# Top-k attention, routed experts and a gated feed-forward on one core: routing operands in one PSUM tile, row scaling a step ahead of its send

## The chip, the core and the metric

The kernel runs on one core of a Trainium2 chip: TensorE (PE, with its weight loads PEld), VectorE (DVE), ScalarE (ACT), GpSimd (POOL) and SyncE (SP, which here issues DMAs only). The metric is the device time in microseconds (us) of one launch. Three runs of the kernel before gave 615.75, 615.82 and 616.0 us; the median is 615.82 us.

## The reference

Three layers follow each other on 1152 tokens (2 batches of 576):

```
scores = q @ k.T / 8                      # 8 heads, head size 64
keep the 32 largest scores of each row, the rest to -1e9
attn = exp(scores - max);  attn /= sum(attn) + 1e-9
x = attn @ v                              # 1152 x 512
logits = x @ w_gate                       # 8 experts
e = argmax(logits);  gate = exp(0) / (sum(exp(logits - max)) + 1e-9)
pos = number of earlier tokens with the same e;  kept while pos < 288
y = relu(x @ w1[e]) @ w2[e] * gate        # 512 -> 1024 -> 512
h = y @ w_in;  out = (h * clip(h + 3, 0, 6) / 6) @ w_out   # 512 -> 2048 -> 512
```

## The kernel before

The attention works on 72 units. A unit is 128 query rows of one head: 9 row tiles `t` times 8 heads `h`, unit `u = 8t + h`. (Row tile 4 is made of the last 64 rows of both batches, so its units have twice as many products with v.) A software pipeline runs 72 steps; step `i` holds stages of several units, and within a step the letters of the string `STEP` give the order in which the instructions are written. Each engine takes its own instructions in that order, so the string is the queue of every engine. The letters that matter here:

- R: `round1(i+1)` and `merge(i-3)` on DVE: the eight largest of each of eight column chunks (L399), and for an older unit the merging of such lists into its 32 largest (L424, L426, L428).
- G: `rest(i)`: on POOL every eighth step the checks of `judge` (L434 to L437), on DVE every fourth step `norm` (L490 to L492: add 1e-9 to the row sum, reciprocal, product with the output of the attention), every eighth step `gate` (L511), and in some steps the parts of the routing.
- L: `round2(i-2)` on DVE (L417), one list over the whole row. It needs POOL's `drop_excess`.
- X, S, B: on POOL `excess(i)` (L405), `shift(i-3)` (L442) and `drop_excess(i-1)` (L413). `excess` of a step waits until `round2` of the step before has let go of its buffer.
- C, Z, F, M, E: on ACT `cut_excess` (L410), `shift_rest` (L447), `fetch` (L383), `below` (L451) and `expo` (L473). `shift` and `shift_rest` write one buffer: POOL takes the first 200 of 576 columns, ACT the other 376.
- T, A, Q: on PE the transposes through PSUM (L466, L467), the products with v (L484), and every second step the scores of two later units (L378). In eight early steps Q also multiplies v by the gate weights (`mix`, L501).
- V: on ACT, the step after a `mix`, the copy of its result into the v tile (`mixed`, L508), and once the copy of the token counts (L549).

When row tiles 0 to 5 are done, `route` gives their tokens an expert. Its parts are spread over steps: `pick` (step 56; L522 to L528), `weigh` and `count` (end of step 57: exp on ACT, 27 small matmuls on PE), `weight + place` (step 59; L552 to L559), and `choose` (steps 58, 60, 61, 62; L232 to L237), which finds the expert with most tokens, so that SP can load its weights. Then `scatter` of one row tile each in steps 60, 63, 66 and 69: ACT scales the rows by their gate (L582), POOL sends them to their places in DRAM (`send_rows`: a memset of a spacer, L154, and an indirect DMA, L155). Row tiles 4 and 5 are scattered behind the loop, with the last units and the routing of tiles 6 to 8. All operands of `route` lie in SBUF, apart from the counts, which TensorE writes to PSUM. PSUM buffers for counts, mixes and attention outputs come from one pool of two (`temp`, tag "o").

After the attention the eight experts and then the feed-forward follow; there the weights stream in on SP and TensorE multiplies.

Of the kernel before, what the change touches and what calls it, by code (L numbers as in the profile page):

```python
# [18 lines left out]
P = 128  # L19
# [16 lines left out]
STEP = "RGLXSCVBTAZFMEQ"  # L36
SPOOL = 200
# [9 lines left out]
CHOOSE = ((2, 0, 1), (4, 1, 1), (5, 2, 2), (6, 4, 2))  # L47
FIRST = 63
# [4 lines left out]
ROUTES = ((0, 6, 56, 3),)  # L53
# [9 lines left out]
def topk_attention_moe_ffn_kernel(ctx, tc, qT, kT, vx, vT, wg, w1, w2, w_in, w_out, out, cap):  # L63
# [20 lines left out]
    def forward(fast):  # L84
# [144 lines left out]
        def choose(sizes_now):  # L229

            v = nc.vector
            return [lambda: v.scalar_tensor_tensor(keys, sizes_now, float(E), rank, op0=OP.mult, op1=OP.add),  # L232
                    lambda: v.max(places, keys),
                    lambda: v.tensor_scalar(sums[:, 0], keys, places[:, 0:1], None, op0=OP.is_equal),
                    lambda: v.tensor_copy(whole[:1, :1], places[:1, :1]),
                    lambda: v.scalar_tensor_tensor(rank, sums[:, 0], float(FRONT), rank, op0=OP.mult, op1=OP.add),
                    lambda: v.tensor_scalar(eids[:, :1], whole[:1, :1], E - 1, E - 1, op0=OP.bitwise_and,  # L237
                                            op1=OP.bitwise_xor)]
# [5 lines left out]
        with ExitStack() as actx:  # L244
# [193 lines left out]

            def shift(u):
                t, h = divmod(u, H)  # L440
                x, top = ubufs[u % 2], tops[t][:, h, 0:1]
                nc.gpsimd.tensor_tensor(x[:, :SPOOL], top.to_broadcast([P, SPOOL]), st[u][:, :SPOOL], op=OP.subtract)  # L442

            def shift_rest(u):
                t, h = divmod(u, H)
                x, top = ubufs[u % 2], tops[t][:, h, 0:1]
                nc.scalar.activation(x[:, SPOOL:S], st[u][:, SPOOL:], AF.Identity, bias=top, scale=-1.0)  # L447

# [65 lines left out]
            def route(t0, t1, direct=False):  # L514
                n = t1 - t0
                r = lambda name, m=E: wk.tile([P, NT, m], F32, name=name, bufs=1)[:, :n]
                mx, dl, el, cand, cm, gt, a, pr = (
                    r("mx", 1), r("dl"), r("el"), r("cand"), r("cm", 1), r("gt", 1), r("ra"), r("pr", 1))
# [12 lines left out]
                pp_of, chosen = [], []  # L531
# [672 lines left out]
```

## Time and profile before

| what | value |
|---|---|
| median of three runs | 615.82 us |
| the profiled execution, its own time | 614.31 us |
| span of its trace | 612.5 us |
| mean granted clock of TensorE in it | 0.988 of full |
| PE busy in the span | 585.3 us (96%) |
| DVE busy | 380.5 us (62%) |
| ACT busy | 358.2 us (58%) |
| POOL busy | 305.2 us (50%) |

The shares mix two stages. Up to about 250 us the attention runs and all engines work; behind that PE works alone and the others wait for it. The start times in the rows below are microseconds from the start of the span; a bracket at the end of a row tells how long the engine was idle before the instruction and what it waited for.

### The profile page before, as it was taken

What the parts mean: (1) busy time and instruction counts of PE and PEld (TensorE: products, weight loads), DVE (VectorE), ACT (ScalarE), POOL (GpSimd) and SP (SyncE); (2) the same over time, 40 slices, a digit from 0 to 9 for tenths busy, and PEclk for the clock granted to TensorE, in tenths of its full rate; (3) what the DMA queues carried; (4) which work ended last, traced back from release to release, by engine and by line L of the source; (5) the groups of instructions that cost most, each with busy time, mean ns of one, the idle gap of its engine ahead of it and who ended that gap; (6) DMA issues with size and microseconds to landing.
All of it is one profiled execution on the core that took longest, in us unless ns stands there. A gap on an engine that the chain in (4) does not pass through costs nothing.

```text
span 612.5 us, 12183 instructions
## 1 busy us (share of the span) xinstructions
PE 585.3 (96%) x4092; PEld 526.2 (86%) x4094; DVE 380.5 (62%) x1793; ACT 358.2 (58%) x689; POOL 305.2 (50%) x374
## 2 busy tenths in 40 slices
PE   8999999999989877999999999999999999999995
PEld 4788888888877666899999999989899999989994
DVE  5999999999999988410463433447655663222221
ACT  4999999988988787212233444546545553242222
POOL 7999999999987799200022323333343232040002
PEclk9999999999997899999999999999999999999998
DMA  8539100100000431585687997522322210020001
GB/s 265 187 104 324 61 18 2 38 2 1 2 2 19 184 127 53 178 322 200 242 315 273 370 350 291 198 67 71 104 79 94 70 35 2 1 103 1 1 1 56
DMA packets 18110, 73.65 MB, mean 120 GB/s; under 512 B 2527, under 2 KB 2783, under 8 KB 15863
## 3 DMA queue, kind: packets, MB, share of 16 engines
q1 hardware_dynamic: 16599, 68.07, 31.6%
q0 software_dynamic: 1440, 4.72, 1.9%
q8 instruction: 34, 0.56, 0.4%
q14 instruction: 37, 0.30, 0.2%
HBM read 63.35 MB, written 9.44 MB: 119 GB/s over the span
## 4 chain that ended last, share of the span: by engine, by line
PE 70%; DVE 24%; POOL 3%; ACT 1%; issue 1%; DVEq 0%; ACTq 0%; POOLq 0%
PE h L1096 16%; PE acc L1110 16%; PE hps L989 12%; PE yps L989 11%; DVE lists L399 7%; PE av L484 6%; DVE lists L417 5%; DVE l L426 4%; PE ps L378 3%; PE pt L466 3%; DVE tops L428 3%; POOL s L413 1%; PE pt L467 1%; PE xp L168 1%; DVE tops L424 1%
## 5 line engine op out<-in xcount | busy, mean ns | idle before, releaser
L399 DVE MAX8 lists<-s 128x8 f32<-128x72 f32 x576 | 118.6, 220 | 3.9 <-ACT s L383 3.9
L484 PE MATMUL av<-vt,pts 128*128 128x96 f32 (+1 forms) x800 | 100.7, 275 | 0.0
L1096 PE MATMUL h<-x2h,fw 128*128 128x384 f32 x384 | 98.2, 337 | 1.1 <-DVE x2l L1007 1.1
L413 POOL TENSOR_TENSOR s<-s,cut 128x576 f32<-128x576 f32 x72 | 92.2, 1281 | 4.1 <-ACT cut L410 3.9
L484 PEld LDWEIGHTS av<-vt,pts 128*128 128x128 f32 (+1 forms) x800 | 92.0, 184 | 2.4 <-issue 0.9
L1110 PE MATMUL acc<-fw,gh 128*128 128x512 f32 x288 | 89.5, 392 | 0.0
L405 POOL TENSOR_TENSOR s<-s,lists 128x576 f32<-128x576 f32 x72 | 83.8, 1165 | 10.4 <-DVE lists L417 7.0
L466 PE MATMUL pt<-ident,ub 128*128 128x128 f32 x355 | 72.5, 290 | 12.4 <-POOL ub L442 7.8
L989 PE MATMUL yps<-hT,wslot 128*128 128x192 f32 (+5 forms) x512 | 78.5, 302 | 0.0
L466 PEld LDWEIGHTS pt<-ident,ub 128*128 128x128 f32 x355 | 50.6, 142 | 32.3 <-POOL ub L442 11.7
L1096 PEld LDWEIGHTS h<-x2h,fw 128*128 128x128 f32 x384 | 70.2, 188 | 5.1 <-DVE x2l L1007 1.3
L989 PEld LDWEIGHTS yps<-hT,wslot 128*128 128x128 f32 x512 | 72.5, 190 | 0.6
L989 PE MATMUL hps<-xe,wslot 128*128 128x192 f32 (+5 forms) x512 | 72.5, 302 | 0.2 <-DVE whole L207 0.2
L989 PEld LDWEIGHTS hps<-xe,wslot 128*128 128x128 f32 x512 | 71.2, 190 | 0.7 <-issue 0.7
L467 PE MATMUL pt<-drop,lb 128*128 128x128 bf16 x355 | 65.7, 222 | 0.0
L1096 PE MATMUL h<-x2l,fw 128*128 128x384 f32 x192 | 64.6, 337 | 0.0
L1110 PEld LDWEIGHTS acc<-fw,gh 128*128 128x128 f32 x288 | 53.4, 188 | 8.2
L1099 ACT ACTIVATE g<-h,three 128x384 f32<-128x384 f32 x48 | 27.9, 581 | 55.6 <-PE h L1096 55.5
L1100 DVE SCALAR_TENSOR_TENSOR g<-g,h 128x384 f32<-128x384 f32 x48 | 26.5, 551 | 54.6 <-ACT g L1099 54.3
L1104 DVE TENSOR_TENSOR gl<-g,gh 128x384 fp32r<-128x384 f32 x48 | 27.4, 571 | 50.5 <-ACT gh L1103 50.5
L1103 ACT CAST gh<-g 128x384 fp32r<-128x384 f32 x48 | 24.6, 513 | 56.5 <-PE acc L1110 51.8
L451 ACT ACTIVATE lb<-s,tops 128x576 bf16<-128x576 f32 x71 | 55.3, 779 | 3.9 <-DVE tops L428 3.2
(429 smaller groups left out, 1060.6 us busy)
## 6 DMA issues: line engine op xcount, KB each, us to landing
wslot<-in_w_dram SPq DMA_DIRECT2D x15, 2048.0 KB, 8.5
raw<-in_w_in_dram SPq DMA_DIRECT2D x16, 512.0 KB, 3.6
raw<-in_w_out_dram SPq DMA_DIRECT2D x16, 512.0 KB, 6.4
xs<-x_tok SPq DMA_DIRECT2D x8, 576.0 KB, 9.4
vt<-in_vx_dram SPq DMA_DIRECT2D x8, 365.0 KB, 4.5
kt<-in_kT_dram SPq DMA_DIRECT2D x8, 288.0 KB, 4.0
vts<-in_vT_dram SPq DMA_DIRECT2D x8, 288.0 KB, 2.9
qt<-in_qT_dram SPq DMA_DIRECT2D x9, 256.0 KB, 5.6
```

The source lines that it names most:

```text
L399: yield lambda c=c: nc.vector.max(lists[t % 2][:, h, c], st[u][:, c * CW:(c + 1) * CW])
L405: nc.gpsimd.tensor_tensor(s2, s, lists[t % 2][:, h, :NCK, KEEP:].to_broadcast([P, NCK, CW]), op=OP.subtract)
L413: nc.gpsimd.tensor_tensor(st2[u], st[u], cuts.pop(u), op=OP.subtract)
L417: nc.vector.max(lists[t % 2][:, h, NCK], st2.pop(u))
L451: nc.scalar.activation(lbufs[u % 2][:, :S], st.pop(u), AF.Relu, bias=tops[t][:, h, TOPK - 1:], scale=-1.0)
L466: nc.tensor.matmul(pt[:, c], ubufs[u % 2][:, cs], ident, is_transpose=True, start=True, stop=False)
L467: nc.tensor.matmul(pt[:, c], lbufs[u % 2][:, cs], drop, start=False, stop=True)
L484: nc.tensor.matmul(av[t, g][rows, h % 4], pts[:, c, cols], vt[b, h // 2][:, at:at + VC], start=c == 0, stop=c == 4)
L989: nc.tensor.matmul(out, wb[:, k], m[:, k, :self.w], start=first and k == 0, stop=last and k == HP - 1)
L1096: nc.tensor.matmul(h2, fw[f][:, 0, a, k * P:(k + 1) * P], (x2h, x2l)[b][:, k, c * CH:(c + 1) * CH], start=n == 0, stop=n == len(ops) - 1)
L1099: nc.scalar.activation(g, h2, AF.Relu, bias=three)
L1110: nc.tensor.matmul(acc[j], g[a][:, j * P:(j + 1) * P], fw[f][:, 1, b], start=f == 0 and n == 0, stop=f == NF - 1 and n == 2)
```

## The change

- `norm` loses its add of 1e-9. The 65th row of the fifth chunk of v, which is padding, gets 1e-9 in the column of ones, and the padding of the transposed buffer gets a zero there, whose exponential is 1.
- In the loop `route` allocates one PSUM tile `board` of a whole bank when it is created, and keeps in it the maxima, the differences `dl`, the candidates, the place sums, the counts, and the operands of `choose` (keys, their maxima, the mark of the largest, its number). `gt`, `el`, `cm` and `ra` stay in SBUF. The two later routings use SBUF as before (`route(..., True)`).
- `route` starts at step 55 in place of 56. `weigh` is issued at the end of step 55, `count` at the end of 56, `weight + place` in step 57, and `choose` two instructions each in steps 58, 59 and 60. The scaling of a row tile comes at the end of steps 57, 60, 63, 66 and 69, its send at the end of the next step; five of the six are now inside the loop.
- `V` stands behind `F` in the order of a step.
- From unit 54 on POOL's `shift` takes 130 columns and ACT's `shift_rest` 446.

```diff
-STEP = "RGLXSCVBTAZFMEQ"
-SPOOL = 200
+STEP = "RGLXSCBTAZFVMEQ"
+SPOOL, SENDS = (200, 130), 54
...
-CHOOSE = ((2, 0, 1), (4, 1, 1), (5, 2, 2), (6, 4, 2))
-FIRST = 63
+CHOOSE = ((3, 0, 2), (4, 2, 2), (5, 4, 2))
+FIRST = 62
...
-ROUTES = ((0, 6, 56, 3),)
+ROUTES = ((0, 6, 55, 3),)
...
-        def choose(sizes_now):
+        def choose(sizes_now, free):
...
-            return [lambda: v.scalar_tensor_tensor(keys, sizes_now, float(E), rank, op0=OP.mult, op1=OP.add),
-                    lambda: v.max(places, keys),
-                    lambda: v.tensor_scalar(sums[:, 0], keys, places[:, 0:1], None, op0=OP.is_equal),
-                    lambda: v.tensor_copy(whole[:1, :1], places[:1, :1]),
-                    lambda: v.scalar_tensor_tensor(rank, sums[:, 0], float(FRONT), rank, op0=OP.mult, op1=OP.add),
+            key, top, this = (free[:, k] for k in range(3))
+            number = free[:1, 2, :1].bitcast(I32)
+            return [lambda: v.scalar_tensor_tensor(key, sizes_now, float(E), rank, op0=OP.mult, op1=OP.add),
+                    lambda: v.max(top, key),
+                    lambda: v.tensor_scalar(this, key, top[:, 0:1], None, op0=OP.is_equal),
+                    lambda: v.scalar_tensor_tensor(rank, this, float(FRONT), rank, op0=OP.mult, op1=OP.add),
+                    lambda: v.tensor_copy(number, top[:1, :1]),
...
+                nc.gpsimd.memset(u[:, S:S + 1], 0.0)
...
-                yield lambda: nc.vector.tensor_scalar(rs, o[:, :, VS - 1:VS], 1e-9, None, op0=OP.add)
-                yield lambda: nc.vector.reciprocal(rs, rs)
+                yield lambda: nc.vector.reciprocal(rs, o[:, :, VS - 1:VS])
...
-                mx, dl, el, cand, cm, gt, a, pr = (
-                    r("mx", 1), r("dl"), r("el"), r("cand"), r("cm", 1), r("gt", 1), r("ra"), r("pr", 1))
+                el, gt, a, cm = r("el"), r("gt", 1), r("ra"), r("cm", 1)
+                if direct:
+                    mx, dl, cand, pr = r("mx", 1), r("dl"), r("cand"), r("pr", 1)
+                else:
+                    board = temp([P, 6 * NT, E], "board")
+                    pp = board[:, :NT]
+                    dl, cand, *ones_of = (board[:, k * NT:k * NT + n] for k in range(1, 5))
+                    mx, pr = (x[:, :, :1] for x in ones_of)
...
-                               *[routes[at][i - at] for _, _, at, _ in ROUTES if i in (at, at + 3)],
+                               *[routes[at][i - at and 3] for _, _, at, _ in ROUTES if i in (at, at + 2)],
...
+                        if i == at:
+                            routes[at][1]()
                         if i == at + 1:
-                            routes[at][1]()
                             routes[at][2]()
-                        n, r = divmod(i - at - 4, gap)
-                        if r == 0 and 0 <= n < b - a:
-                            scatter(a + n)
-                            sent = a + n + 1
+                        n, r = divmod(i - at - 2, gap)
+                        if 0 <= n < b - a and r < 2:
+                            if r == 0 and i < NU - 1:
+                                rows[a + n] = wk.tile([P, DM], F32, name="xg", bufs=4)
+                                scale(a + n, rows[a + n])
+                            elif r == 1:
+                                send(a + n)
+                                sent = a + n + 1
...
+        vx[64, :, 4, (h + 1) * VS - 1] = 1e-9
```

How the change moves instructions shows at three places. The first is DVE's queue in the kernel before around step 61, where a `norm` meets two instructions of `choose` (`sums` marks the expert with most tokens):

```order
L428 MAX tops<-l_3373 128x8
L490 TENSOR_SCALAR rs<-av 128x4
L491 RECIPROCAL rs<-rs 128x4
L234 TENSOR_SCALAR sums<-keys,places 128x8
L492 TENSOR_TENSOR x_tok<-av,rs 128x288
L235 CAST whole<-places 1x1
```

In the changed kernel the same engine has a `norm` together with the six instructions of `weight + place` in step 57 (line numbers are those of the changed file):

```order
L562 TENSOR_REDUCE gt<-el 128x6
L563 TENSOR_SCALAR gt<-gt 128x6
L496 RECIPROCAL rs<-av 128x4
L564 RECIPROCAL gates<-gt 128x6
L567 SCALAR_TENSOR_TENSOR ra<-board,oh 128x48
L568 TENSOR_REDUCE board<-ra 128x6
L497 TENSOR_TENSOR x_tok<-av,rs 128x288
L569 SCALAR_TENSOR_TENSOR dest<-cm,board 128x6
```

The mark of the largest is gone from this norm (it stands with one neighbour in step 59), and the six instructions of `weight + place`, two steps earlier, share a step with a norm of one instruction less.

The second place is POOL's queue around the first send, in the kernel before (steps 59 to 61):

```order
L437 COPY rest_ok<-tops 128x8
L405 TENSOR_TENSOR s_3289<-s,lists_115 128x576
L442 TENSOR_TENSOR ub_203<-tops,s 128x200
L413 TENSOR_TENSOR s_3227<-s,cut 128x576
L405 TENSOR_TENSOR s_3335<-s,lists_115 128x576
L442 TENSOR_TENSOR ub_207<-tops,s 128x200
L413 TENSOR_TENSOR s_3289<-s,cut 128x576
L154 MEMSET spacer 1x1
L155 DMA xs<-xg,dest 9216x512
L405 TENSOR_TENSOR s_3396<-s,lists_115 128x576
```

And in the changed kernel (steps 57 to 59):

```order
L408 TENSOR_TENSOR s_3171<-s,lists_115 128x576
L448 TENSOR_TENSOR ub_203<-tops,s 128x130
L416 TENSOR_TENSOR s_3084<-s,cut 128x576
L408 TENSOR_TENSOR s_3222<-s,lists_115 128x576
L448 TENSOR_TENSOR ub_208<-tops,s 128x130
L416 TENSOR_TENSOR s_3171<-s,cut 128x576
L154 MEMSET spacer 1x1
L155 DMA xs<-xg,dest 9216x512
L437 TENSOR_TENSOR over<-lists_114 128x64
```

The first send has moved ahead of the checks of step 59, two steps earlier, and the shifts are narrower.

The third place is ACT's queue around a copy of a `mix` (`vt<-mix`), before:

```order
L410 ACTIVATE cut<-s_747 128x576
L508 COPY vt_126<-mix 128x8x8
L508 COPY vt_126<-mix 64x2x8
L447 ACTIVATE ub_207<-s,tops 128x376
L383 ACTIVATE s<-ps 128x576
L451 ACTIVATE lb_209<-s,tops 128x576
L473 ACTIVATE pts<-pt 128x640
```

And after:

```order
L413 ACTIVATE cut<-s_748 128x576
L453 ACTIVATE ub_208<-s,tops 128x376
L386 ACTIVATE s<-ps 128x576
L513 COPY vt_126<-mix 128x8x8
L513 COPY vt_126<-mix 64x2x8
L457 ACTIVATE lb_211<-s,tops 128x576
L479 ACTIVATE pts<-pt 128x640
```

The copies stand two activations later, and still ahead of the exponential (`pts<-pt`) of the same step.

## Rows read from the trace of the kernel before

**Rows 1.** The page: busy tenths of PE in 40 slices, the chain by engine.

```profile
PE   8999999999989877999999999999999999999995
...
PE 70%; DVE 24%; POOL 3%; ACT 1%; issue 1%; DVEq 0%; ACTq 0%; POOLq 0%
```

**Rows 2.** Windows: length, busy of PE, PEld, DVE, ACT, POOL (counts), PE clock, DMA.

```profile
120.00:140.00 20.00, 20.00 (x204) 16.61 (x202) 19.88 (x136) 17.47 (x32) 18.77 (x24) 1.00 0.01 2
...
186.00:191.00 5.00, 5.00 (x24) 3.75 (x23) 4.90 (x28) 4.53 (x9) 4.87 (x8) 0.50 0.00 0
...
222.00:232.00 10.00, 6.61 (x60) 5.97 (x60) 7.94 (x50) 7.92 (x14) 9.82 (x12) 1.00 0.01 2
```

**Rows 3.** Timeline of DVE: round2 of four steps (start, length, engine, line).

```profile
58.21 0.75 DVE L417 MAX8 lists<-s 128x8 f32<-128x576 f32 x1
...
82.83 0.75 DVE L417 MAX8 lists<-s 128x8 f32<-128x576 f32 x1
...
94.88 0.75 DVE L417 MAX8 lists<-s 128x8 f32<-128x576 f32 x1
...
119.17 0.75 DVE L417 MAX8 lists<-s 128x8 f32<-128x576 f32 x1
```

**Rows 4.** Timeline of DVE: the start of one norm.

```profile
168.59 0.15 DVE L490 TENSOR_SCALAR rs<-av 128x4 f32<-128x4 f32 x1
168.78 0.18 DVE L491 RECIPROCAL rs<-rs 128x4 f32<-128x4 f32 x1
```

**Rows 5.** Waits from 20 to 170 us: engine, line, waited for, total, times, longest.

```profile
ACT vt L508 <- PE mix L501: 3.4, 6, 0.7
DVE rs L490 <- PE av L484: 2.6, 3, 1.4
```

**Rows 6.** Timeline of DVE: instructions of routing and choice.

```profile
178.23 0.76 DVE L523 SCALAR_TENSOR_TENSOR dl<-L,mx 128x48 f32<-128x48 f32 x1
...
186.26 0.15 DVE L232 SCALAR_TENSOR_TENSOR keys<-pos_p,rank 128x8 f32<-128x8 f32 x1
...
189.37 0.24 DVE L553 TENSOR_SCALAR gt<-gt 128x6 f32<-128x6 f32 x1
...
189.76 1.18 DVE L557 SCALAR_TENSOR_TENSOR ra<-pos,oh 128x48 f32<-128x48 f32 x1
...
197.28 3.33 DVE L234 TENSOR_SCALAR sums<-keys,places 128x8 f32<-128x8 f32 x1
...
203.77 0.90 DVE L236 SCALAR_TENSOR_TENSOR rank<-sums,rank 128x8 f32<-128x8 f32 x1
...
240.74 1.00 DVE L528 TENSOR_TENSOR oh<-cand,cm 128x16 bf16<-128x16 f32 x1
```

**Rows 7.** Timeline of POOL beside them.

```profile
189.59 1.28 POOL L413 TENSOR_TENSOR s<-s,cut 128x576 f32<-128x576 f32 x1
...
197.69 1.17 POOL L405 TENSOR_TENSOR s<-s,lists 128x576 f32<-128x576 f32 x1
198.81 0.52 POOL L442 TENSOR_TENSOR ub<-tops,s 128x200 f32<-128x200 f32 x1
199.29 1.28 POOL L413 TENSOR_TENSOR s<-s,cut 128x576 f32<-128x576 f32 x1
...
219.79 0.99 POOL L155 DMA_INDIRECT xs<-xg,dest  x1 [0.16 <-issue]
...
240.55 1.15 POOL L744 TENSOR_TENSOR ub<-tops,s 128x576 f32<-128x576 f32 x1
```

**Rows 8.** Waits from 170 to 240 us, POOL's two.

```profile
POOL s L405 <- DVE lists L417: 5.9, 5, 1.5
...
POOL xs L155 <- DVE tops L428: 2.9, 2, 1.5
```

**Rows 9.** Timeline of ACT: a late shift.

```profile
206.06 0.61 ACT L447 ACTIVATE ub<-s,tops 128x376 f32<-128x376 f32 x1 [0.24 <-DVE tops L424]
```

**Rows 10.** Timeline of PE: the products with v of one unit.

```profile
185.34 2.39 PE L484 MATMUL av<-vt,pts 128*128 128x96 f32 x10
```

More of the change, by code (lines that the diff above doesn't have):

```diff
@@ L437, in judge, with spool @@
                 g.tensor_copy(rest_ok[:, 1, t], thr[:, :, 0])
+            def spool(u):
+                return SPOOL[u >= SENDS]
             def shift(u):
                 t, h = divmod(u, H)
-                x, top = ubufs[u % 2], tops[t][:, h, 0:1]
-                nc.gpsimd.tensor_tensor(x[:, :SPOOL], top.to_broadcast([P, SPOOL]), st[u][:, :SPOOL], op=OP.subtract)
+                x, top, n = ubufs[u % 2], tops[t][:, h, 0:1], spool(u)
+                nc.gpsimd.tensor_tensor(x[:, :n], top.to_broadcast([P, n]), st[u][:, :n], op=OP.subtract)
             def shift_rest(u):
                 t, h = divmod(u, H)
-                x, top = ubufs[u % 2], tops[t][:, h, 0:1]
-                nc.scalar.activation(x[:, SPOOL:S], st[u][:, SPOOL:], AF.Identity, bias=top, scale=-1.0)
+                x, top, n = ubufs[u % 2], tops[t][:, h, 0:1], spool(u)
+                nc.scalar.activation(x[:, n:S], st[u][:, n:], AF.Identity, bias=top, scale=-1.0)
             def below(u):
@@ L529, in route @@
                 ]
-                pp_of, chosen = [], []
+                at, chosen = [pos[:, sl]], []
                 def count():
-                    pp = temp([P, NT, E], "pos_p")
-                    pp_of.append(pp)
+                    to = temp([P, NT, E], "pos_p") if direct else pp
                     for t in range(t0, t1):
                         for j in range(t):
-                            nc.tensor.matmul(pp[:, t], ones, oh[:, j], start=j == 0, stop=False)
-                        nc.tensor.matmul(pp[:, t], tri, oh[:, t], start=t == 0, stop=True)
+                            nc.tensor.matmul(to[:, t], ones, oh[:, j], start=j == 0, stop=False)
+                        nc.tensor.matmul(to[:, t], tri, oh[:, t], start=t == 0, stop=True)
+                    if not direct:
+                        for j in range(t1):
+                            nc.tensor.matmul(to[:, t1], ones, oh[:, j], start=j == 0, stop=j == t1 - 1)
+                        chosen.extend(choose(to[:, t1], board[:, 5 * NT:5 * NT + 3]))
+                    at[0] = to[:, sl]
                     if direct:
-                        at[0] = pp[:, sl]
                         copy()
-                    else:
-                        for j in range(t1):
-                            nc.tensor.matmul(pp[:, t1], ones, oh[:, j], start=j == 0, stop=j == t1 - 1)
-                        chosen.extend(choose(pp[:, t1]))
-                at = [pos[:, sl]]
-                copy = lambda: nc.scalar.copy(pos[:, sl], pp_of[0][:, sl])
+                copy = lambda: nc.scalar.copy(pos[:, sl], at[0])
                 weigh = lambda: nc.scalar.activation(el, dl, AF.Exp)
@@ L583, in scale, with send @@
                                      scale=gates[:, t])
+            rows = {}
+            def send(t):
+                scat.append(send_rows(t, rows.pop(t)))
             def scatter(t):
-                xg = wk.tile([P, DM], F32, name="xg", bufs=4)
-                scale(t, xg)
-                scat.append(send_rows(t, xg))
+                if t not in rows:
+                    rows[t] = wk.tile([P, DM], F32, name="xg", bufs=4)
+                    scale(t, rows[t])
+                send(t)
             def all_in_order():
@@ L762, in in_steps @@
                 nc.scalar.copy(plain[:, :DM // 2].rearrange("p (h d) -> p h d", d=D), x_tok[:, t, :4, :D])
-                nc.vector.tensor_scalar(rs, o[:, :, VS - 1:VS], 1e-9, None, op0=OP.add)
-                nc.vector.reciprocal(rs, rs)
+                nc.vector.reciprocal(rs, o[:, :, VS - 1:VS])
                 nc.vector.tensor_tensor(x_tok[:, t, 4:, D:], o[:, :, D:VS - 1], rs.to_broadcast([P, 4, E]), op=OP.mult)
```

6 lines of the change are left out of this document (3 added, 3 removed).

## The prediction

> **What bounds the kernel now.** I read the page's slices and its chain first. PE is at least nine tenths busy in every slice from the seventeenth to the last but one and holds 70% of the chain; DVE holds 24%, nearly all of it in the attention [rows 1]. The change touches only the attention, up to 250 us. What follows is PE work without gaps, so I take every microsecond won or lost at the end of the attention to arrive at the end of the span.
>
> Then the windows. In the attention no engine is alone: from 120 to 140 us PE is busy for all 20 us and DVE for 19.88 (row tile 4, whose products with v are double). From 222 to 232 us POOL is busy for 9.82 of 10, DVE for 7.94, ACT for 7.92 [rows 2]. So the bound moves: DVE in general, PE in row tile 4, POOL at the end.
>
> DVE's pace is read from `round2` (L417), once a step. Eight steps take 24.62 us while `mix` runs (58.21 to 82.83) and 24.29 us behind it (94.88 to 119.17) [rows 3]. Eight steps hold two norms and one gate, some 1.7 us, so a bare step is 2.82 us. POOL's step is the excess (1.12 from its start to the shift's), the shift (0.48) and the drop (1.25): 2.85 us [rows 7], with sends and checks on top. The two are nearly equal, so a stall of one is made up only where the other waits.
>
> The stretch from 178 to 211 us is the one that matters. Small DVE instructions of the routing take many times their length there: L523 0.76 us, L557 1.18, L234 3.33, L236 0.90, while L232, which reads its counts from PSUM, takes 0.15 [rows 6]. L557 starts inside a POOL drop (189.59 for 1.28) and ends 0.07 us behind it. L234 starts before an excess and ends 0.04 us behind the drop that follows it, at 200.57 [rows 7]. A DVE instruction with all its tensors in SBUF here waits until POOL pauses; one with a PSUM operand does not. POOL in turn waits for DVE: its idle time before the excess is 5.9 us in five waits, and 2.9 us in two waits ahead of a send, whose row scaling ACT has not done [rows 8]. That is 8.8 us of POOL idle, and behind 211 us POOL never catches up.
>
> [...]
>
> **The change part by part.**
>
> *Adds of the norm.* L490 to L491 is 0.19 us [rows 4]; the reciprocal now reads PSUM, and by L232 against its neighbours that costs nothing visible. I count 0.19 per norm, only where DVE bounds. In steps 9 to 28 it goes with the moved copies (next). In steps 29 to 36 two norms: 0.4. In row tile 4 PE bounds: nothing, for what DVE saves it waits for PE (over the whole stretch L490 waits 2.6 us in three waits [rows 5]), save the one behind the last wait: 0.2. In steps 46 to 54 two norms, 0.4, but POOL, at 8 x 2.85 = 22.8 us and a set of checks in eight steps, stands close behind DVE's 23.9: I take 0.25. Together 0.85.
>
> *Copies of the mixes later.* ACT waits 3.4 us in six waits for PE's mix [rows 5] with the shift, the fetch and the exponential behind it; PE then waits for the exponential. After the move the shift and the fetch fill that wait. The eight steps could go from 24.62 to 24.29 - 2 x 0.19 = 23.9, 0.7 us in eight steps, over some 20 steps 1.7; if PE or ACT keeps the pace, 0. All engines then lie within 0.3 us of each other in four steps, so I take 1.2.
>
> *Routing and choice on PSUM.* POOL's idle time after the change, step by step. Step 55: five pick instructions at 0.2 each put DVE's round2, and POOL's next excess, 1.0 later. Step 57: 2.82 + norm 0.58 + six instructions at 0.2 = 4.6. One of the six, L563 (before: L553), is an add of SBUF to SBUF and still waits for POOL. Before it took 0.24, for POOL happened to pause [rows 6]; now POOL has its drop ready, and I find it 0.65 into that drop, so 0.65 us more (bounds 0 and 2.3, the rest of a whole POOL step). 5.25 against 2.74 of POOL: idle 2.4. Steps 58 on: choose costs 0.2 to 0.3 a step, and POOL, with sends, is the slower one. Idle together 3.4 instead of 8.8: 5.4 won.
>
> *Scaling a step ahead.* ACT scales as often as before, but by my count of the steps two to four us before POOL comes to the send. The waits of 2.9 us are in the 8.8. What is queued behind a send on POOL is the excess or the checks.
>
> *Five sends in the loop instead of four* before the last unit's drop: one send is 0.09 + 0.16 + 0.99 [rows 7], 1.2 us lost on POOL.
>
> *Narrow shift.* 200 columns take 0.52 us and 576 take 1.15 [rows 7], 1.68 ns a column, so 70 columns are 0.12 us; steps 57 to 71 save 15 x 0.12 = 1.75 us of POOL. ACT's shift of 376 columns takes 0.61 [rows 9], so its 70 more cost 0 to 0.11. ACT is busy for 7.92 us where POOL is for 9.82 [rows 2]: 2 us in ten are free, and 0.1 in a step of three is hidden by POOL; without that cover 15 x 0.1 = 1.5 us.
>
> *Board takes a PSUM buffer two steps earlier.* In step 57 the products with v must now wait for that step's norm; by the same count PE stands for about 3 us. PE has slack there, but before, behind the token counts, it ran at half clock from 186 to 191 us, ten products in 2.39 us [rows 2, 10]. A late exponential would hold ACT's cut and POOL's drop: 0 to 2.0 us lost, I take 0.65.
>
> *Tail.* The add of the last norm: 0.2 won. L528 waits behind POOL's full shift (240.55 + 1.15; 1.00 us [rows 6, 7]). That shift no longer follows a send, and the interleaved chain is one link shorter, so now an earlier link (`dl`) meets it: 0, bounds 0.9 won and 0.2 lost.
>
> *The two memsets of one column* fall before POOL has a unit to work on, and `FIRST` moves loads that come 50 us ahead of the first expert: nothing.
>
> Sum: 5.4 + 1.75 - 1.2 + 0.85 + 1.2 - 0.65 + 0.2 = 7.5 us won. The profiled execution took 614.31 us, so 606.8; the median of the runs is 1.5 above it, so 608.3 us.
>
> About eleven of the moved instructions now take a source from PSUM. [...]
>
> **The rivals.**
>
> 1. *The stall moves to the add that stayed in SBUF.* L563 meets a POOL that runs without a pause: L234 shows 3.3 us of such a wait. For it: its operands. Against: POOL's next excess waits for a round2 that stands behind L563, so POOL must pause within one step. With the upper bound, 1.65 more than counted, and 0 from the mix copies: 7.5 - 1.65 - 1.2 = 4.65, 611.2 us.
>
> 2. *More is won.* L563 slips between two POOL instructions (0.65), dl misses the shift (0.9), the mix stretch gives 1.7 (0.5 more), PE keeps its clock (0.65): 10.2 us, 605.6.
>
> 3. *The change does not do what it says*: POOL was the true bound before too. Then only its own queue counts: 1.75 - 1.2, and 0.2 in the tail: 0.75 won, 615.1. Against it: the 8.8 us of idle time.
>
> 4. *Slower: PE at half clock.* The pause in step 57 lets the clock fall and the small products of a step keep it there. At half clock a step is ten products at 2.39, about as much for the scores every second step, and for the ten matmuls of the transposes, which are shorter, I take 1.6: 5.2 us against POOL's 3.2 (2.74, a third of a send, an eighth of the checks). Each slow step costs 2.0; against the 8.15 won without clock loss, it decides from the fifth slow step. Six cost 12: 619.7 us. For it: clock 0.50 in 186 to 191. Against: it lasted about two steps, and in 222 to 232 PE is idle for a third of the time at full clock [rows 2].
>
> **How the numbers follow.** My forecast, 608.3, has a chance of 0.56 (606.5 to 610.3: clock, tail and mix copies each part of the way to their bounds). Rival 1: 0.20, rival 2: 0.11, rival 3: 0.06, rival 4: 0.07. The range of 605.2 to 612.6 takes in rivals 1 and 2 and leaves out 3 and 4 and part of the ends. Within 0.2% (1.2 us) is about what a measurement of this kernel cannot tell from no change. Faster by more: 0.56 + 0.20 + 0.11 = 0.87; the same: 0.06; slower: 0.07.
>
> **What would show it.** Right, if in the profile after the instruction that marks the largest key takes under 0.25 us, POOL's idle time before the excess and the sends falls below 4 us, no send waits for its scaling, and POOL's full shift starts 6 to 9 us earlier than 240.55 us [rows 7]. L563 at 0.5 to 1.0 us shows that term; above 1.5 is rival 1. Eight steps near 24.0 between 55 and 85 us show the copies; 24.6 shows that PE holds them. A clock at half for over 10 us between 180 and 215 us is rival 4. The forecast is wrong if POOL is busy without a pause from 185 us on and that shift still comes less than 4 us earlier, or if the time behind the attention changes by more than 1 us.

## The result and the profile after

The changed kernel takes 609.48 us (median of four runs, 608.93 to 609.91), the kernel before beside it 615.91 us (615.75 to 616.38): a ratio of 0.9894, 95% interval 0.9877 to 0.9911, 6.4 us won. The forecast was 608.3 us. The profiled execution of the changed kernel took 609.91 us with a span of 608.0 us. Two runs of the experiments at a mean granted clock of 0.557 and 0.655 (967.70 us of e3, 827.16 us of the kernel before) are left out of what follows.

The page after, busy tenths of PE and the chain by engine, answers to [rows 1]:

```profile
PE   8999999999989888999999999999999999999994
...
PE 75%; DVE 17%; POOL 5%; issue 1%; ACT 1%; DVEq 0%; POOLq 0%; ACTq 0%
```

DVE's part of the chain falls from 24% to 17% and PE's grows. Lines have moved: `round2` is now L420, the excess L408, the drop L416, the pick L534 to L540, the gates' sum L562 to L564, the places L567 to L569, the mark of the largest key L236.

Windows of the kernel after, columns as in [rows 2]:

```profile
58.00:82.00 24.00, 24.00 (x214) 20.57 (x212) 23.72 (x158) 23.16 (x45) 23.49 (x28) 1.00 0.25 80
...
120.00:140.00 20.00, 20.00 (x203) 16.61 (x202) 19.30 (x126) 17.47 (x31) 18.80 (x23) 1.00 0.01 2
...
181.00:186.00 5.00, 2.96 (x15) 2.87 (x16) 4.73 (x30) 3.19 (x7) 2.44 (x4) 0.61 0.00 0
```

From 58 to 82 us, where the mixes run, PE is now busy for all 24 us. In the kernel before, the same window read:

```profile
58.00:82.00 24.00, 23.69 (x212) 20.31 (x208) 23.79 (x157) 22.82 (x44) 23.50 (x28) 1.00 0.27 83
```

PE had 0.31 us to spare there, and the change used it up. `round2` of the four steps that answer to [rows 3], on DVE's timeline:

```profile
58.00 0.75 DVE L420 MAX8 lists<-s 128x8 f32<-128x576 f32 x1
...
82.32 0.75 DVE L420 MAX8 lists<-s 128x8 f32<-128x576 f32 x1
...
94.18 0.75 DVE L420 MAX8 lists<-s 128x8 f32<-128x576 f32 x1
...
118.10 0.75 DVE L420 MAX8 lists<-s 128x8 f32<-128x576 f32 x1
```

Eight steps take 24.32 us in the stretch of the mixes (24.62 before) and 23.92 behind it (24.29 before). The waits from 20 to 170 us that answer to [rows 5]:

```profile
ACT s L386 <- PE ps L381: 5.9, 10, 0.9
...
DVE rs L496 <- PE av L490: 3.6, 5, 1.6
```

The six waits for the mix are gone, and ACT waits for PE's scores instead: 2.5 of these 5.9 us lie between 20 and 90 us, where the kernel before had no such wait. DVE waits 1.0 us longer than before for the products with v, 0.8 of it behind 90 us. What DVE saved in row tile 4 turned into that wait.

Routing and choice on DVE's timeline, against [rows 6]:

```profile
174.39 0.21 DVE L535 SCALAR_TENSOR_TENSOR board<-L,board 128x48 f32<-128x48 f32 x1
...
181.12 0.59 DVE L563 TENSOR_SCALAR gt<-gt 128x6 f32<-128x6 f32 x1
...
181.85 0.17 DVE L567 SCALAR_TENSOR_TENSOR ra<-board,oh 128x48 f32<-128x48 f32 x1
...
188.80 0.22 DVE L236 TENSOR_SCALAR board<-board 128x8 f32<-128x8 f32 x1
...
233.90 1.06 DVE L537 SCALAR_TENSOR_TENSOR cand<-dl,desc 128x16 f32<-128x16 f32 x1
```

0.76, 1.18 and 3.33 us have become 0.21, 0.17 and 0.22. The first and the last of them ran beside a busy POOL; the 0.17 fell into a pause of POOL (181.68 to 183.71), so that e8 below has to show what it takes beside one. The add of the gates (L563), which stayed in SBUF, takes 0.59. In the tail the stall of 1.00 us at `oh` has become one of 1.06 at `cand`, an earlier link of the same chain.

POOL's timeline beside them, against [rows 7]:

```profile
180.40 1.28 POOL L416 TENSOR_TENSOR s<-s,cut 128x576 f32<-128x576 f32 x1
183.71 1.17 POOL L408 TENSOR_TENSOR s<-s,lists 128x576 f32<-128x576 f32 x1 [2.02 <-DVE lists L420]
...
185.77 1.28 POOL L416 TENSOR_TENSOR s<-s,cut 128x576 f32<-128x576 f32 x1 [0.53 <-ACT cut L413]
...
233.79 1.15 POOL L765 TENSOR_TENSOR ub<-tops,s 128x576 f32<-128x576 f32 x1 [0.16 <-DVE dl L535]
```

And POOL's waits from 170 to 240 us, against [rows 8]:

```profile
POOL s L408 <- DVE lists L420: 2.7, 2, 2.0
...
POOL xs L155 <- ACT xg L592: 0.4, 1, 0.4
```

5.9 us before the excess have become 2.7, and of 2.9 us before the sends 0.4 remains, before a send behind the full shift. The wait of 0.53 for the cut is new, as are 0.21 us for a later cut and 0.74 for DVE ahead of the last narrow shift. Counted whole, from the shift of unit 52 to the full one, POOL sits idle for 9.5 of 66.2 us before and for 5.3 of 60.1 after (windows, before first, columns as in [rows 2]):

```profile
174.31:240.55 66.24, 53.54 (x449) 45.71 (x447) 62.12 (x362) 55.09 (x94) 56.78 (x73) 0.92 0.21 81
```

```profile
173.64:233.79 60.15, 50.67 (x448) 44.16 (x446) 56.01 (x352) 54.09 (x94) 54.90 (x73) 0.94 0.24 93
```

So 4.2 of the 6.1 us won there are idle time, and 1.9 are work that POOL no longer does. L563 ends (181.71) 0.03 us behind the end of the drop at 180.40: it waited for POOL as the others had. The full shift starts at 233.79, 6.8 us earlier. Of the clock, against [rows 2, 10], the products with v:

```profile
183.04 2.42 PE L490 MATMUL av<-vt,pts 128*128 128x96 f32 x10 [2.22 <-DVE dest L569]
186.85 2.31 PE L490 MATMUL av<-vt,pts 128*128 128x96 f32 x10
```

PE pauses for 2.22 us and runs two units at about half clock (0.61 in the window above), then at full clock. The first matmul of the first expert, the milestone that the rest of the text uses, on PE's timeline:

```profile
249.39 10.64 PE L1009 MATMUL hps<-xe,wslot 128*128 128x192 f32 x64 [0.20 <-DVE whole L207]
```

In the profile before it starts at 255.68 us, 6.3 us later. From there to the end of the last matmul both profiles take the same time, 349.77 us before and 349.78 after. The last matmuls, before and after:

```profile
605.07 0.39 PE L1110 MATMUL acc<-fw,gl 128*128 128x512 f32 x1
```

```profile
598.78 0.39 PE L1130 MATMUL acc<-fw,gl 128*128 128x512 f32 x1
```

What lies behind them is 7.07 us before and 8.79 after, and 7.77 in a second profile of the kernel after (e12). So the spans of the two profiles (612.52 and 607.96 us) are only 4.6 us apart, where the medians are 6.4 apart.

### The profile page after: what moved, and what is told of

It reads as the page before. It is cut to its first block, busy times and chain, and to the rows that moved or that the text cites. A ratio compares the mean times of both kernels' runs of the same rounds, so it can differ in the third digit from the quotient of the medians.

```text
span 608.0 us, 12169 instructions
## 1 busy us (share of the span) xinstructions
PE 583.1 (96%) x4092; PEld 525.0 (86%) x4094; DVE 374.2 (62%) x1775; ACT 357.9 (59%) x689; POOL 303.3 (50%) x376
## 4 chain that ended last, share of the span: by engine, by line
PE 75%; DVE 17%; POOL 5%; issue 1%; ACT 1%; DVEq 0%; POOLq 0%; ACTq 0%
PE h L1116 17%; PE acc L1130 16%; PE hps L1009 12%; PE yps L1009 12%; PE av L490 7%; DVE lists L402 5%; PE ps L381 4%; DVE lists L420 4%; PE pt L472 3%; DVE l L429 3%; POOL s L416 2%; DVE tops L431 2%; PE pt L473 1%; PE pt L646 1%; POOL s L408 1%
## 5 line engine op out<-in xcount | busy, mean ns | idle before, releaser
L416 POOL TENSOR_TENSOR s<-s,cut 128x576 f32<-128x576 f32 x72 | 92.7, 1288 | 4.5 <-ACT cut L413 4.2
L408 POOL TENSOR_TENSOR s<-s,lists 128x576 f32<-128x576 f32 x72 | 84.4, 1173 | 6.6 <-DVE lists L402 3.3
```

The costliest lines, as they stand in the source:

```text
L408: nc.gpsimd.tensor_tensor(s2, s, lists[t % 2][:, h, :NCK, KEEP:].to_broadcast([P, NCK, CW]), op=OP.subtract)
L416: nc.gpsimd.tensor_tensor(st2[u], st[u], cuts.pop(u), op=OP.subtract)
```

## The experiments

Single runs of one kernel lie up to 5 us apart here, more than most parts of the change are worth; places in the trace repeat far better. (A good part of the scatter lies at the two ends: in the 14 profiles the first shift starts at 15.3 to 16.5 us, and behind the last matmul there are 7.1 to 8.8 us.) So each profile is also read by POOL's shifts, one for each of the 72 units, counted from the first shift of the same profile, and by the first matmul of the first expert. The table gives them as differences to the kernel after (its own: units 36, 52, 56, 60 and 71 at 123.72, 173.64, 190.45, 202.85 and 233.79 us, the first shift at 15.61, the matmul at 249.39). Medians are of four to six runs, ratios against the kernel before on the same chip; the kernel after has 0.9894.

| kernel | us | ratio to before, interval | u36 | u52 | u56 | u60 | u71 | first matmul |
|---|---|---|---|---|---|---|---|---|
| before | | 1 | +0.77 | +0.97 | -1.08 | +4.22 | +7.06 | +6.59 |
| e8_psum_alone | 611.48 | 0.9919, 0.9906–0.9933 | +0.79 | +1.06 | -1.56 | +1.19 | +2.77 | +3.43 |
| e1_sbuf | 611.25 | 0.9920, 0.9907–0.9933 | +0.01 | +0.03 | +0.32 | +1.63 | +1.66 | +1.67 |
| e3_wide_shift | 611.17 | 0.9923, 0.9910–0.9937 | +0.02 | +0.04 | +0.11 | +0.34 | +1.53 | +1.54 |
| e2_scale_late | 610.50 | 0.9916, 0.9902–0.9931 | -0.01 | +0.03 | +1.48 | +1.26 | +1.29 | +1.30 |
| e4_copies_early | 612.04 | 0.9936, 0.9922–0.9949 | +1.04 | +1.06 | +2.12 | +2.38 | +2.42 | +3.50 |
| e5_norm_add | 609.73 | 0.9893, 0.9875–0.9910 | +0.18 | +0.19 | +0.60 | +0.79 | +0.78 | +1.51 |
| e6_gate_sum | 610.01 | 0.9904, 0.9889–0.9918 | -0.03 | 0.00 | -0.47 | -0.70 | -0.69 | -0.68 |
| e7_tail_psum | 610.76 | 0.9908, 0.9891–0.9925 | -0.02 | +0.01 | -0.42 | -0.66 | -0.67 | +0.63 |
| e9_pos_later | 609.65 | 0.9888, 0.9869–0.9907 | +0.02 | +0.06 | -0.99 | +1.31 | +1.34 | +1.45 |
| e10_pos_tail | 607.88 | 0.9862, 0.9844–0.9879 | -0.02 | +0.01 | -1.00 | -1.25 | -1.25 | -2.11 |
| e11_narrower | 607.95 | 0.9875, 0.9851–0.9900 | +0.01 | +0.03 | -1.06 | -1.57 | -2.02 | -2.01 |
| e12_after_again | 609.61 | 0.9896, 0.9879–0.9912 | -0.03 | -0.01 | -0.02 | +0.16 | +0.15 | +0.16 |

The last row is the same kernel in another profile: up to unit 56 places repeat within 0.04 us, behind it within 0.17.

**Operands back in SBUF (e1).** The theory that the waits on small instructions were the loss, against the order alone.

```diff
...
-                    dl, cand, *ones_of = (board[:, k * NT:k * NT + n] for k in range(1, 5))
-                    mx, pr = (x[:, :, :1] for x in ones_of)
+                mx, dl, cand, pr = r("mx", 1), r("dl"), r("cand"), r("pr", 1)
...
+                    three_of = wk.tile([P, 3, E], F32, name="free", bufs=1)
...
-                        chosen.extend(choose(to[:, t1], board[:, 5 * NT:5 * NT + 3]))
+                        chosen.extend(choose(to[:, t1], three_of))
```

> The kernel after with the routing's and the choice's operands back in SBUF (only the counts stay in PSUM); its order, its narrow shift and its early scaling are kept. Theory (the gain of steps 53 to 71 comes from small vector instructions that no longer wait through GpSimd's instructions): rows of about 1 us or more come back at dl, cand, ra, pr, dest or the comparison of keys, GpSimd's idle time over 5 to 14 us between 170 and 206 us grows again to 6 to 8 us from 3.6, the first expert's first matmul starts 2.5 to 5 us later than at 249.4, and the time is 612 to 614.5 against 609.5 after and 615.9 before. Rival (it is the new order of the sends alone that took the idle time away): the matmul starts within 0.8 us of 249.4 and the time is 609.3 to 610.3.

DVE's timeline and POOL's waits (170 to 240 us) of this kernel:

```profile
174.70 1.13 DVE L532 SCALAR_TENSOR_TENSOR dl<-L,mx 128x48 f32<-128x48 f32 x1
...
190.02 2.75 DVE L236 TENSOR_SCALAR free<-free 128x8 f32<-128x8 f32 x1
```

```profile
POOL s L408 <- DVE lists L420: 4.8, 4, 2.0
```

The waits return at `dl` and at the mark, POOL idles 2.1 us longer before its excess, and 1.67 us are lost: more than the rival allows, less than the 2.5 to 5 expected. Of the instructions put back in the loop only these two met a busy POOL. The 1.67 us are a net figure. The place sums are back in SBUF too, so ACT's copy of the counts no longer waits for DVE's last routing instruction, and POOL's waits for the cut fall from 0.7 to 0.2 us. And PE kept its full clock in this profile, after a pause of 2.29 us:

```profile
181.00:186.00 5.00, 2.71 (x27) 2.43 (x28) 4.76 (x31) 4.18 (x9) 2.97 (x4) 1.00 0.00 0
```

**Operands alone on the kernel before (e8).** After's `route` and `choose` in the kernel before; order, widths, sends and norms as they were.

> The kernel before with one part of the change alone: the routing's and the choice's operands in one PSUM tile, with the counts read where they were added up. The order, the wide shift, the scaling at the send and the two instructions of the norm stay as before. Theory (the port waits were most of the idle time before the sends): the waits of 1.18, 3.33, 0.90 us are gone, GpSimd's idle time between 170 and 220 us falls from about 8.8 us to 5 or 6, the first expert's first matmul starts 2.5 to 4 us earlier than at 255.7, and the time is 611.5 to 613.5. Rival (without the new order the sends still wait for the gather of dest and for the scaled rows, so nothing is won): the matmul starts within 1 us of 255.7 and the time is 615 to 616.

What the expectation calls port waits was seen only by its times: in the kernel before L523, L557, L234 and L236 end 0.02 to 0.07 us behind the end of a POOL drop, and no run shows a port. Against the kernel before the shift of the last unit starts 7.06 - 2.77 = 4.3 us earlier, the first matmul 3.2 us. The time is at the edge of the theory's range. Here the product that took 1.18 us (`ra`) meets a POOL drop, as in the kernel before, and takes 0.17 (DVE, then POOL):

```profile
189.41 0.17 DVE L564 SCALAR_TENSOR_TENSOR ra<-board,oh 128x48 f32<-128x48 f32 x1
```

```profile
189.24 1.28 POOL L415 TENSOR_TENSOR s<-s,cut 128x576 f32<-128x576 f32 x1
```

One wait of a send for its scaled row is still there (POOL's waits, 170 to 240 us; ACT's scaling ends at 195.59, the send starts at 195.89):

```profile
POOL xs L155 <- DVE rs L492: 1.8, 1, 1.8
```

So the operands are worth 1.7 us where the rest of the change is in and 4.3 where it is not: much of the idle time could be had in either way. The ratios say the same: the operands alone win 0.81%, all the rest without them 0.80%, both together 1.06%. The tail of this run lost 1.1 us to a half clock (below).

**Shift as wide as before (e3).** `SPOOL, SENDS = (200, 200), 54`.

> The kernel after with the late shifts as wide on GpSimd as before (200 columns in every step, not 130 from step 54). Theory (GpSimd sets the pace of steps 54 to 71, 18 shifts, each of 70 columns more): 1.3 to 2.2 us are lost, all of them after 180 us, the time is 610.8 to 611.7. Rival A (ScalarE, 10.00 of 10 us busy from 206 us on in the kernel after, is as much the bound): the time stays within 0.6 us of 609.5. Rival B (ScalarE is the bound and 130 is too narrow): 0.5 to 1.5 us are won, 608 to 609.

1.54 us lost, growing by 0.11 to 0.13 a unit from unit 59 to 69. POOL sets the pace there; rivals A and B fall.

**Scaling in the step of the send (e2).** The early `scale` is left out, `scatter(a + n)` scales and sends.

> The kernel after with the rows scaled in the step of their send, as before, not a step ahead. Theory (each send then waits for its scaled rows: two such rows of 1.5 and 1.4 us stood in the kernel before, on GpSimd, which has no slack there): 1.0 to 3 us of idle time of GpSimd with ScalarE's scaling as its releaser come back between 183 and 225 us, the first expert's first matmul starts 1 to 3 us after 249.4, and the time is 610.5 to 612.5. Rival (the scaling is done before GpSimd gets to the send anyhow): the waits for the scaled rows are under 0.5 us in all, and the matmul starts within 0.5 us of 249.4.

On POOL's timeline the first send shows it:

```profile
189.00 1.16 POOL L155 DMA_INDIRECT xs<-xg,dest  x1 [2.26 <-DVE lists L402]
```

What the send lacked is the row that ACT scales: that instruction ran from 187.99 to 188.70 us, so the releaser named in the row is not the one. It cost 1.5 us at unit 56, and no later send waited over 0.4 us. 1.30 us in all, at the low end of the theory, which had more than one such wait.

**Gate copies at their earlier place (e4).**

```diff
-STEP = "RGLXSCBTAZFVMEQ"
+STEP = "RGLXSCVBTAZFMEQ"
```

> The kernel after with the gate copies back at their earlier place in ScalarE's step. Theory by the trace after (TensorE itself bounds the steps with the mixes: it waits for nothing from 20 to 90 us, eight steps take 24.3 us, not 23.9; the later copies gave the 0.3 us between 24.62 and 24.32): eight steps from 58 us take 24.45 to 24.65 us, and the start of row tile 4 comes 0.3 to 0.8 us later; the time is 609.7 to 610.3. Rival (the copies' place costs nothing; the 0.3 us came from the shorter norm): eight steps stay at 24.3 us and all starts within 0.15 us of the kernel after.

Eight steps on DVE's timeline take 24.64 us, as the theory has it:

```profile
58.44 0.75 DVE L420 MAX8 lists<-s 128x8 f32<-128x576 f32 x1
...
83.08 0.75 DVE L420 MAX8 lists<-s 128x8 f32<-128x576 f32 x1
```

By unit 36 1.04 us are lost, the copies' whole worth in that stretch. Neither theory had what came at unit 56, 1.06 us more. The letter V also places ACT's copy of the token counts. First ACT's row, then POOL's:

```profile
183.97 0.20 ACT L559 COPY pos<-board 128x48 f32<-128x48 f32 x1 [2.91 <-DVE dest L569]
```

```profile
187.79 1.28 POOL L416 TENSOR_TENSOR s<-s,cut 128x576 f32<-128x576 f32 x1 [1.63 <-ACT cut L413]
```

That copy waits for DVE's last routing instruction on the shared tile; at the earlier place the shift, the fetch, a mask, an exponential, a scaling and then the cut are queued behind it, and POOL waits 1.1 us more for the cut.

**Add of the norm back (e5).** Two instructions in the loop's norm, as in the kernel before.

> The kernel after with the addition of 1e-9 back in the norm (two instructions of VectorE in place of one, in 17 norms before the tail; the data still holds the 1e-9). Theory (VectorE's saved instruction counts only where VectorE or a norm's product is late: my sum gave it 0.85 us): 0.5 to 1.1 us are lost, in steps 46 to 54 and in the first 30 steps, none in row tile 4 but 0.2 after its last wait; the time is 610 to 610.6. Rival A (VectorE bounds nearly every step outside row tile 4: 17 times 0.18 us): 2 to 3 us lost. Rival B (TensorE and GpSimd hide it all): under 0.3 us.

0.78 us by the last shift, as much as expected, but not where: 0.18 up to row tile 4, where it vanishes (-0.02 at unit 40), 0.19 at unit 52, and the rest in the steps around the first send, to which the theory gave nothing. The 0.73 more at the first matmul is mostly clock (below). The medians do not show the loss: 609.73 us, a ratio of 0.9893.

**Gates' sum in PSUM (e6).** One line: `gt = ones_of[0][:, :, 1:2]`.

> The kernel after with the sum of the gates (gt) moved to the same PSUM tile too. Theory (the row of 0.59 us of adding 1e-9 to gt is a wait for GpSimd): the row falls to about 0.2 us and the first expert's first matmul starts 0.2 to 0.5 us earlier than at 249.4; the time is 609.0 to 609.4. Rival (what follows it waits for something else anyhow): the row is shorter and nothing else moves, the time is 609.4 to 609.7.

```profile
181.64 0.17 DVE L564 TENSOR_SCALAR board<-board 128x6 f32<-128x6 f32 x1
```

That is the add, on DVE's timeline. 0.59 has become 0.17, and 0.47 us are won by unit 56, 0.70 by unit 60. The second part came with the clock: PE's pause is 1.8 us here, not 2.2, and one unit runs at half clock, not two. In the kernel after the scores behind the second slow unit come late and POOL's drop waits for the cut (ACT, then POOL):

```profile
190.42 0.65 ACT L386 ACTIVATE s<-ps 128x576 f32<-128x576 f32 x1 [1.25 <-PE ps L381]
```

```profile
196.51 1.28 POOL L416 TENSOR_TENSOR s<-s,cut 128x576 f32<-128x576 f32 x1 [0.21 <-ACT cut L413]
```

Neither wait is there in e6. The median (610.01) doesn't show the gain; its interval holds the kernel after's.

**Tail in PSUM (e7), on e6.** The tail's first `mx`, `dl` and `cand` in columns 384 to 432 of the PSUM tile that holds the products of heads 0 to 3.

> The kernel after with the sum of the gates in PSUM (measured before: 0.5 us) and, in the tail, the first routing's maximum, difference and candidates in unused columns of a PSUM tile that is there anyhow. Theory (the wait of 1.06 us at cand in the tail stands on the path to the first expert): cand takes about 0.2 us, the first expert's first matmul starts 1.0 to 1.6 us before 249.4, and the time is 607.9 to 608.6. Rival (as the stall moved from dl to cand by the change, it moves on to the next small instruction, or what follows waits for GpSimd's last shift anyhow): cand is short, but the matmul starts only 0.4 to 0.6 us earlier, as with the gates alone.

`cand` takes 0.17 us, and DVE has all that follows done 0.9 us earlier. But ACT's exponential of `dl` now reads that tile, and waits for DVE's last instruction on it:

```profile
235.95 0.18 ACT L571 ACTIVATE el<-av 128x16 f32<-128x16 f32 x1 [1.55 <-DVE x_tok L503]
```

With e6's 0.68 won before it, the tail loses 1.3, so for the matmul neither theory nor rival holds. Some 0.3 of it is that wait (the products of the last unit start at 240.70, in the kernel after at 240.38, the last shifts at 233.78 and 233.79). The rest is PE's clock at the last selection matmuls and the filler behind them, on PE's timeline:

```profile
247.94 1.36 PE L188 MATMUL ps<-wslot 128*128 128x192 f32 x4 [0.65 <-DVE xe L174]
```

In the kernel after those four take 0.92 us.

**Counts' copy a step later (e9, on e6), and cand with its addend in PSUM, dl in SBUF (e10, on e9).** The last three lines are e10's, of the tail alone; `base` gets a copy of `desc`.

```diff
-                                if i == at + 2:
+                                if i == at + 3:
                                     routes[at][5]()
...
+                    if at_psum is not None:
+                        cand = at_psum[:, :n * E].rearrange("p (n e) -> p n e", e=E)
+                        base = at_psum[:, n * E:n * E + E]
```

> The kernel after with the sum of the gates in PSUM (0.68 us won up to the last shift, measured before) and ScalarE's copy of the counts one step later. Theory (the copy waits 1.81 us, in ScalarE's queue ahead of a mask, an exponential, a scaling and the cut bits, for VectorE's last routing instruction on the same PSUM tile; the 0.53 us that GpSimd waits for the cut bits in that step hang on it): that wait of GpSimd goes, the last shift starts 1.0 to 1.3 us before that of the kernel after, counted from the first shift, the first expert's first matmul as much. Rival (VectorE's own queue bounds that step, as the 2.02 us that GpSimd waits for VectorE there say): 0.6 to 0.8 us, as with the gates alone.

> The one before, and in the tail only the candidates and a copy of their addend in unused columns of a PSUM tile; the difference, which ScalarE reads, stays in SBUF. Theory (the run that moved the difference as well had cand at 0.17 us and everything behind it on VectorE 0.9 us earlier, but ScalarE's exponential of the difference waited 1.55 us for VectorE's last instruction on that PSUM tile): cand takes 0.2 us, the exponential starts within 0.3 us of its old distance to the last shift, the time from the last shift to the first expert's first matmul falls from 15.6 to 14.6 to 15.0 us. Rival (another wait on that path, or TensorE at half clock in the last selection matmuls as in that run, takes it): 15.3 to 16.9 us.

Both win 1.0 us at unit 56, the wait of 0.53 for the cut is gone, and e10 keeps 1.25 to the last shift, as the theory of e9 has it. Their code is the same up to the tail, and yet e9's own profile loses 2.5 us against e10's between units 57 and 59, so that its last shift misses the theory. A window of e9, and the one of e10:

```profile
186.00:191.00 5.00, 5.00 (x24) 3.94 (x22) 4.97 (x34) 2.70 (x5) 4.79 (x10) 0.50 0.13 52
```

```profile
186.00:191.00 5.00, 5.00 (x44) 4.23 (x43) 4.94 (x32) 4.28 (x8) 4.78 (x10) 0.94 0.14 52
```

In e9 PE stayed at half clock for a second unit and its scores, which came late; in e10 for one unit only. ACT's timeline of e9:

```profile
191.44 0.65 ACT L386 ACTIVATE s<-ps 128x576 f32<-128x576 f32 x1 [2.57 <-PE ps L381]
```

ACT's cut and POOL's drop stand behind it. Then the tail of e10, DVE and ACT:

```profile
233.24 0.17 DVE L548 SCALAR_TENSOR_TENSOR av<-dl,av 128x16 f32<-128x16 f32 x1
```

```profile
233.66 0.20 ACT L571 ACTIVATE el<-dl 128x16 f32<-128x16 f32 x1
```

`cand` starts 0.16 us into the full shift and no longer waits, with `dl` in SBUF and its addend in PSUM; `el` has no wait. From the last shift to the first matmul it is 14.74 us, 15.60 in the kernel after. During a full shift of 1.15 us on POOL `cand` took 0.17 us here, and 1.06 in the kernel after, where it has both inputs and its result in SBUF.

**Late shifts of 90 columns (e11), on e9.**

> The first one (gates in PSUM, counts' copy later) with the late shifts of 90 columns on GpSimd, not 130. Theory (ScalarE, 10.00 of 10 us busy from 206 us on, is by now as much the bound as GpSimd): the last shift stays within 0.3 us of that of the first one. Rival (GpSimd alone bounds: from 200 to 130 columns each of the last 14 shifts gave 0.11 us): another 0.7 to 1.0 us are won.

Against e10, whose loop is the same but for the width, unit 71 comes 0.77 us earlier: the rival holds, and ACT, though busy for 10.00 of 10 us from 206 us on in the kernel after, was not yet the bound.

**The kernel after once more (e12).**

> The kernel after once more, unchanged, as the measure for the three others on the same chip: 609.0 to 610.0 us; shifts and first matmul within 0.1 us of the first profile, counted from the first shift.

609.61 us, and the places within 0.17, not 0.1. The best of these, e10, takes 607.88 (606.52 to 608.32) beside it: 1.7 us less by the medians, 2.1 to 2.3 by the traces; the intervals of the two ratios just touch. e11's width in e10 was not tried.

## Why the prediction was right, and where its sizes were off

The time came 1.2 us above the forecast, within its range, and by the mechanism named. Its size is in part luck, since errors of both signs cancel. By its own steps, counted in the profiles (forecast 7.5 us, 6.59 at the first matmul):

- *Up to row tile 4* the copies of the mixes and the norms were to give 1.2 + 0.4; 0.77 came (unit 36). This is the step that failed most. 23.9 us for eight steps supposed that PE had room. It was busy for 23.69 of 24 us there, a row that I had not read; by it eight steps could fall to 24.62 x 23.69 / 24 = 24.3 us, and 24.32 came. "If PE or ACT keeps the pace, 0" was the bound that held for the rest. e4 and e5 split it: undoing the copies alone costs 1.04, undoing the norm's step alone 0.18, together more than the 0.77.
- *Row tile 4:* the DVE time saved there went into DVE's wait for PE (2.6 to 3.6 us), as forecast.
- *Norms in all:* 0.85 forecast, 0.78 by e5 to the last shift. The sum agrees by luck: all 0.85 were put ahead of step 55, where e5 shows 0.19; the other 0.59 came around the first send.
- *From unit 52 to the last shift:* 5.4 + 1.75 - 1.2 - 0.65 = 5.3 forecast, 7.06 - 0.97 = 6.09 came. Up to the last two drops it was 5.6, counted from the first shifts at 15.31 and 15.61 us. POOL's idle time in step 57 was 2.0 (2.4 forecast, though its own 5.25 - 2.74 is 2.5). Of the 8.8, 2.7 are left before the excess and none before a send of the loop, and 0.7 before the cut are new: 3.4, as forecast. The narrow shift gave 1.54 (1.75). The other 0.5 was not forecast. In the kernel before, the fifth send stands between these drops and the full shift, so the 1.2 us forecast as a loss come back there, less 0.9 us of new idle time (0.74 + 0.16). POOL before, then after:

```profile
235.88 2.51 POOL L413 TENSOR_TENSOR s<-s,cut 128x576 f32<-128x576 f32 x2
...
239.06 0.99 POOL L155 DMA_INDIRECT xs<-xg,dest  x1 [0.16 <-issue]
```

```profile
229.62 2.51 POOL L416 TENSOR_TENSOR s<-s,cut 128x576 f32<-128x576 f32 x2
...
233.22 0.41 POOL L448 TENSOR_TENSOR ub<-tops,s 128x130 f32<-128x130 f32 x1 [0.74 <-DVE tops L427]
```

- *L563:* 0.59 us, the wait of the forecast (0.65 added to 0.2 would be 0.85); e6 shows that it cost 0.5 us, or 0.7 with the clock that came with it. Rival 1, which had 1.65 more there, is out.
- *Clock:* PE paused 2.2 us in step 57 (3 forecast) and ran two units at half clock. Of the 0.65 us forecast for this, 0.2 can be seen, the wait of 0.21 in e6's section; what the first slow unit cost no run isolates. What a late score costs when the half clock lasts one unit longer, e9 shows: 2.5 us, close to the 2.0 of a slow step in rival 4. It did not get six such steps in any profile, and that the small products of a step hold the clock down, as it has it, no run shows.
- *Tail:* 0.2 + 0 forecast, -0.47 came, outside its bound of 0.2 lost. I had the stall move to `dl`; it moved to `cand`, 0.34 us later in the chain, and what I missed is that two links (`cm`, `oh`) are then still to come behind the end of POOL's shift, where before `oh` itself was stalled. e10 takes the stall away and the 0.86 us come back.
- *Rival 3* (POOL the bound before too) is out: e8 wins 4.3 us to the last shift without shortening POOL's work.
- *Behind the attention:* a change of more than 1 us there was to be a sign of a wrong forecast, and the two profiles do differ by 1.7 us. It is not the change: up to the last matmul they agree within 0.01 us, and behind it the same kernel differs by 1.0 us between two profiles (8.79 and 7.77). The sign was set finer than one profile can tell.
- *Sends:* I put both waits of 2.9 us down to rows not scaled yet, and in the kernel before both sends do start 0.3 us behind the end of their scaling. With the late scaling only one returns (e2), and with the operands alone one is left (e8): in the other the scaling itself was late, on an ACT that had waited 2.5 us for DVE behind the mark of the largest key. The sum of both was right. ACT in the kernel before:

```profile
202.18 0.61 ACT L447 ACTIVATE ub<-s,tops 128x376 f32<-128x376 f32 x1 [2.54 <-DVE tops L424]
```

- *The rule of the operands* (all in SBUF: the instruction waits for POOL) is too wide. In the kernel before it held for SCALAR_TENSOR_TENSOR (L523 0.76 us, L557 1.18, L236 0.90), TENSOR_TENSOR (L528 1.00) and TENSOR_SCALAR (L234 3.33). Between L553 and L557 a reciprocal from SBUF to SBUF ran inside the very drop that held L557 up and did not wait:

```profile
189.65 0.19 DVE L554 RECIPROCAL gates<-gt 128x6 f32<-128x6 f32 x1
```

Small rows of TENSOR_REDUCE and MAX8 beside POOL's work stay at 0.2 us too (L522 0.18 and L428 0.21 us inside the drop at 177.63, before), and the two TENSOR_REDUCEs that now write to PSUM took 0.18 and 0.20 us before and 0.20 and 0.21 after: moving those gained nothing.

What stays open: why PE returns to full clock after one unit in some profiles and later in others (after a pause of 1.8 us one unit in e6, e7, e10 and e11 and two in e9; after 2.2 us two in the kernel after, e2 and e12; after 2.29 us none in e1), and why in the profiles of e4, e5, e7 and e8 the clock of the last 4 us before the first expert's first matmul is 0.64 to 0.70 (0.7 to 1.1 us at that matmul) and 1.00 in the others. Nor is the earlier start of `route` tested by itself: every run on the kernel after keeps it.

## What to carry to other kernels

A small VectorE instruction of the kinds that waited here, beside a GpSimd that runs without a pause, can be priced by what GpSimd has queued, not by its size: 3.33 us for a mark on 8 columns. With one of its two inputs in PSUM that price was gone here (`ra` 0.17 us inside a drop in e8, 1.18 before), but keep in SBUF what ScalarE reads: in e7 it waited 1.55 us for VectorE's last use of the same PSUM tile. Where four engines are within a few per cent of each other (22.82 to 23.79 of 24 us from 58 us on, before), look up the busiest engine's time in each stretch before you credit a saved instruction: here the same 0.19 us counted in one stretch and vanished in the next. When runs scatter more than the effect, compare places in the trace, counted from an early common event.

## What the runs showed of the hardware

- With all operands in SBUF the mark of the largest key waited through an excess, a shift and a drop of GpSimd in a row, 2.75 us in e1 and 3.33 us before. The instruction on the same data in PSUM took 0.22 beside GpSimd's checks (after). A reciprocal, SBUF to SBUF, took 0.19 inside a drop (before).
- With one input in PSUM, the other and the result in SBUF, `ra` took 0.17 us inside a GpSimd drop of 1.28 us (e8). With one input and the result in PSUM, `cand` took 0.17 us inside a GpSimd shift of 1.15 us (e10).
- The same instructions at the same place ran with a granted clock of 0.50 in one profile and 0.94 in another, after a pause of PE of 1.8 us in both (e9, e10).
